# Batch 1's queries through scratch in device memory, its keys mixed two positions at a time, output weights in three tiles

## The chip, the cores and the metric

The kernel runs on one core of a Trainium2 chip. The metric is device time in microseconds (us) of one execution of the whole program; lower is better. A profile is one execution recorded by the hardware profiler, with the start and end of each engine's instructions. The engines are TensorE (PE in the profile; PEld is its weight load), VectorE (DVE), ScalarE (ACT), GpSimd (POOL) and SyncE (SP). SP computes nothing here and issues transfers; Pool issues others. Transfers run on 16 DMA engines that all queues share.

## What is computed

Four batches of eight heads, 768 positions, 64 channels a head. The positions of a head are cut into eight blocks of 96. An 8x8 matrix per head, made from `sort_net` by five rounds of normalising, mixes the blocks of keys and of values; then each block of queries attends to its own mixed block. The result, 3,072 rows of 512, goes through a gated feed-forward network.

```python
for _ in range(5):
    P = np.exp(P - np.max(P, axis=-1, keepdims=True))
    P = P / (np.sum(P, axis=-1, keepdims=True) + 1e-09)
    P = P / (np.sum(P, axis=-2, keepdims=True) + 1e-09)
k_sorted = np.einsum('bhij,bhjcd->bhicd', P, k_b)
v_sorted = np.einsum('bhij,bhjcd->bhicd', P, v_b)
scores = scale * np.matmul(q_b, k_sb.transpose(0, 1, 2, 4, 3))
attn = softmax(scores)
x = np.matmul(attn, v_sb)          # then 3072 x 512
g = x @ w_gate
out = (g / (1 + np.exp(-g)) * (x @ w_val)) @ w_out
```

## The kernel before

Matrix work is in bfloat16 with float32 sums. The feed-forward network goes in eight stages `ffn(0)` to `ffn(7)`, each over half a batch (384 rows): 12 gate tiles (line 385) and 12 value tiles (line 403) of four matmuls each, and, from stage 1 on, the output matmuls of the stage before (line 420, `outp`). The attention of the batches that follow is woven in: `merge` takes the stage's own steps in order, adds up a cost given to each by hand (0.65 or 0.87), and puts each side step in as soon as the sum has reached its due number. The order of TensorE and Pool is written out this way, so TensorE works strictly in order: what stands behind a waiting matmul waits too.

Batch 0 is done ahead of stage 0, by hand, and partly in stage 0. Batch 1 comes in stage 1: values mixed (`v_chunk`), keys and queries brought into channel-by-position form (`kq_chunk`, line 238), then `units(1, ...)`: each unit is the scores of two heads and half of the blocks (`scores`, line 293, matmuls on line 307), exponentials, attention times values, and the turn of the result. Units 0 to 3 of batch 1 stand in stage 1, units 4 to 7 in stage 2. Batches 2 and 3 form a pair whose keys are mixed together in stage 2.

How keys and queries of a batch get their form differs:

- Batch 0 loads one tile `qk0`: half of it holds keys with two positions of a block in the two halves of the partitions (`k0`), so one matmul mixes two positions (`k0_chunk`, 48 positions x 2 matmuls); queries are turned by a selecting matrix (`q0_chunk`).
- Batch 1 loads keys into the upper 64 partitions and queries into the lower 64 of one tile (`load_k(1)`, `load_q(1)`, lines 160 and 161). `kq_chunk` multiplies each of 96 positions by a matrix `rmix[1]` which holds the mix in its upper rows and an identity in its lower rows (line 536): 96 x 2 matmuls in chunks of 16 positions, six drains of 128x1024 from PSUM to `kqt`, by VectorE and ScalarE in turn. Keys and queries both come out in `kqt`.
- Batches 2 and 3 use `kq_chunk` for their keys alone. Their queries are copied by a casting transfer into scratch in device memory, 768 rows of 512 (`q_cast`, line 370), and brought back by one transposing transfer a batch on SP's queue (`q_dma`, line 375).

All large loads are issued by Pool in an order written out in lines 144 to 162: values and batch 0, gate and value weights in steps of 256 columns, values of batch 1, keys and queries of batch 1, and last the output weights as one transfer into one tile `wo_sb` (line 162). Pool then copies batch 1's values into another layout (line 124), and issues the loads of batches 2 and 3. SP's queue carries, in this order of use, the results (line 427), the transposing transfers of attention results from batch 1's unit 4 on (`x_dma`, line 366), and `q_dma`.

The score matmuls take their keys and queries from these places:

```python
k_sb, k_at, q_sb, q_at = ((kqts[b], 0, kqts[b], GI * C) if b < 2 else
                          (kqts["p"], (b - 2) * GI * C, kqts["q"], (b - 2) * GI * C))
```

Of the kernel before, what the change touches and what calls it, by code (L numbers as in the profile page):

```python
# [10 lines left out]
BF16 = mybir.dt.bfloat16  # L11
# [6 lines left out]
def kernel(  # L18
# [25 lines left out]
    R = H * NB  # L44

    k_nat = k.rearrange("b h (j c) d -> b (h j) c d", c=C)
    q_nat = q.rearrange("b h (j c) d -> b (h j) c d", c=C)
    v_nat = v.rearrange("b h (j c) d -> b (h j) c d", c=C)
    sn = sort_net.rearrange("b h i j -> (b h) i j")
    wg_dram = moe_w_gate.rearrange("(kc p) f -> p kc f", p=128)  # L50
# [1 line left out]
    wo_dram = moe_w_out.rearrange("(mc p) f -> p mc f", p=128)  # L52

    const = ctx.enter_context(tc.tile_pool(name="const", bufs=1))
    natp = ctx.enter_context(tc.tile_pool(name="natp", bufs=2))
    vnp = ctx.enter_context(tc.tile_pool(name="vnp", bufs=1))
    kqp = ctx.enter_context(tc.tile_pool(name="kqp", bufs=2))
    vtp = ctx.enter_context(tc.tile_pool(name="vtp", bufs=2))
# [12 lines left out]

    wg_sb = wpool.tile([128, NKC, DF], BF16)
    wv_sb = wpool.tile([128, NKC, DF], BF16)
    wo_sb = wpool.tile([128, NFC, DM], BF16)
    vch = const.tile([128, D * C + 32], BF16)
    nc.vector.memset(vch[:, D * C:], 0.0)
    vch3 = vch[:, 0:D * C].rearrange("p (d c) -> p d c", c=C)
# [2 lines left out]

    dram = ctx.enter_context(tc.tile_pool(name="dram", bufs=1, space=bass.MemoryType.DRAM))
    q_scr = [dram.tile([S, H * D], BF16, name=f"q_scr{b}") for b in range(2, B)]
    kq_tiles = {}
    v_tiles = {}

    def kq_tile(b):
        if b not in kq_tiles:
            kq_tiles[b] = natp.tile([128, C, D], BF16, name=f"kq{b}", tag="nat")
        return kq_tiles[b]

    def load_k(b, lo, hi):
        rows = highr if b else lowr
        nc.gpsimd.dma_start(out=kq_tile(b)[rows, lo:hi, :], in_=k_nat[b, :, lo:hi, :])

    def load_k_pair():
        kq_tiles["p"] = natp.tile([128, C, D], BF16, name="kp", tag="nat")
        for u in range(2):
            nc.gpsimd.dma_start(out=kq_tiles["p"][u * R:(u + 1) * R], in_=k_nat[2 + u])

    def load_q(b, lo, hi):  # L100
        rows = lowr if b else highr
        nc.gpsimd.dma_start(out=kq_tile(b)[rows, lo:hi, :], in_=q_nat[b, :, lo:hi, :])

    def load_v(b, lo, hi):
        if b // 2 not in v_tiles:
# [29 lines left out]
    halves = (lowr, highr)  # L135
    qk0 = natp.tile([128, C, D], BF16, name="qk0", tag="nat")
    k0 = qk0[:, 0:HC, :]
    q0 = [qk0[:, HC + t * QC:HC + (t + 1) * QC, :] for t in range(2)]
    q_runs = q.rearrange("b h (t r c) d -> b t r h (c d)", t=2, c=QC)

# [16 lines left out]
    load_v(1, 0, C)  # L157
    for m in range(1024, DF, 256):
        load_gv(m, m + 256)
    load_k(1, 0, C)  # L160
    load_q(1, 0, C)
    nc.gpsimd.dma_start(out=wo_sb, in_=wo_dram)

    rmix = {b: const.tile([128, 2, H, NB], BF16, name=f"rmix{b}") for b in (0, 1, "p")}
    for t in rmix.values():
# [62 lines left out]
    def kqt_tile(b):  # L228
        if b not in kqts:
            kqts[b] = kqp.tile([128, 2 * H2 * NB * C + 32], BF16, name=f"kqt{b}", tag="kqt")  # L230
        return kqts[b]
# [3 lines left out]
    def chunk_tile(name, n, tag):  # L235
        return pair_tile(name, tag) if n == 2 else bank_tile(name, tag)

    def kq_chunk(b, at, n, eng, tag):
        dst = kqt_tile(b)[:, 0:2 * GI * C].rearrange("p (n c) -> p n c", c=C)
        rm = rmix[b].rearrange("p a (g two) i -> p two (a g) i", two=2)  # L240
        tp = chunk_tile("tkq", n // 8, tag).rearrange("p (l n) -> p l n", n=2 * GI)
        for lc in range(n):
            for two in range(2):
                nc.tensor.matmul(tp[two * D:(two + 1) * D, lc, :],  # L244
                                 lhsT=kq_tiles[b][:, at + lc, :],
                                 rhs=rm[:, two], start=True, stop=True)
        drain(eng, dst[:, :, at:at + n], tp.transpose([0, 2, 1]))

# [6 lines left out]
                                 rhs=sel[:, two], start=True, stop=True)  # L255
        drain(eng, dst[:, :, :, at:at + n], tp.rearrange("p l g r -> p g r l"))

    def k0_chunk(at, n, eng, tag):
        dst = kqt_tile(0)[:, 0:GI * C].rearrange("p (n a c) -> p a n c", a=2, c=HC)
        rm = rmix[0].rearrange("p a (g two) i -> p two a g i", two=2)  # L260
        tp = chunk_tile("tk0", n // 8, tag).rearrange("p (l a n) -> p l a n", l=n, a=2)
        for lc in range(n):
            for two in range(2):
                nc.tensor.matmul(tp[two * D:(two + 1) * D, lc].rearrange("p a (g i) -> p a g i", g=H2),
                                 lhsT=k0[:, at + lc, :], rhs=rm[:, two], start=True, stop=True)
        drain(eng, dst[:, :, :, at:at + n], tp.rearrange("p l a n -> p a n l"))

    def v_chunk(b, at, n, eng, tag):
# [23 lines left out]

    def scores(b, u, tag):
        half, g = divmod(u, H2)
        k_sb, k_at, q_sb, q_at = ((kqts[b], 0, kqts[b], GI * C) if b < 2 else
                                  (kqts["p"], (b - 2) * GI * C, kqts["q"], (b - 2) * GI * C))
        if tag == "gen":
            wide = None
            pss = [bank_tile("qk"), bank_tile("qk")]
        else:  # L300
            wide = pair_tile("qk", tag).rearrange("p (two n) -> p two n", two=2)
            pss = [wide[:, 0], wide[:, 1]]
        for i4 in range(4):
            at = (g * NB + half * 4 + i4) * C
            for two in range(2):
                lo = two * D
                nc.tensor.matmul(pss[two][:, i4 * C:(i4 + 1) * C],  # L307
                                 lhsT=k_sb[lo:lo + D, k_at + at:k_at + at + 128],
                                 rhs=q_sb[lo:lo + D, q_at + at:q_at + at + C],
                                 start=True, stop=True)  # L310
        return wide, pss
# [11 lines left out]
    def qk(b, u, tag="b"):  # L323
        exps(b, u, *scores(b, u, tag))
# [44 lines left out]
    def q_cast(b):  # L369
        nc.gpsimd.dma_start(out=q_scr[b - 2].rearrange("s (h d) -> s h d", d=D),  # L370
                            in_=q[b].rearrange("h s d -> s h d"))

    def q_dma(b):
        dst = kqt_tile("q")[:, (b - 2) * GI * C:(b - 1) * GI * C]
        nc.sync.dma_start_transpose(out=dst.rearrange("p (g s) -> p g s", g=H2), in_=q_scr[b - 2])
# [37 lines left out]
    def outp(n, t3, part):  # L413
        b, half = divmod(n, 2)
        h_w = h_tiles[n]
        if part == 0:
            o_tiles[n] = bank_tile("o_ps", "x" if 2 <= n < 2 * B - 1 or n == 2 * B - 1 and t3 == 1 else "gen")
        o_ps = o_tiles[n]
        for m in range(part * 4, part * 4 + 4):
            nc.tensor.matmul(o_ps, lhsT=h_w[:, m, ts(t3, 128)], rhs=wo_sb[:, m, :],  # L420
                             start=(m == 0), stop=(m == NFC - 1))
        if part < 2:
            return
        o_sb = opool.tile([128, DM], FP32, name="o_sb", tag="o_sb")
        nc.scalar.copy(o_sb, o_ps)  # L425
        base = b * S + half * TW + t3 * 128
        nc.sync.dma_start(out=out[ds(base, 128), :], in_=o_sb)

    def out_halves(n, t3):
        b, half = divmod(n, 2)  # L430
        base = b * S + half * TW + t3 * 128
        for part, eng in ((0, "s"), (1, "v")):
            cols = slice(part * DM // 2, (part + 1) * DM // 2)
            o_ps = bank_tile("o_ps")[:, 0:DM // 2]
            for m in range(NFC):
                nc.tensor.matmul(o_ps, lhsT=h_tiles[n][:, m, ts(t3, 128)], rhs=wo_sb[:, m, cols],  # L436
                                 start=(m == 0), stop=(m == NFC - 1))
            o_sb = opool.tile([128, DM // 2], FP32, name="oh_sb", tag="oh_sb")
            drain(eng, o_sb, o_ps)
            nc.sync.dma_start(out=out[ds(base, 128), cols], in_=o_sb)  # L440
# [26 lines left out]
    def mix_rows(dst, rows, b):  # L467
        nc.vector.tensor_tensor(dst, mask[rows].unsqueeze(2).to_broadcast([R, H, NB]),
                                w_ps[rows, :, b].transpose([0, 2, 1]), op=ALU.mult)
# [9 lines left out]
    v_chunk(0, 32, 8, "v", "gen")  # L479
    v_chunk(0, 40, 16, "s", "b")  # L480
    v_chunk(0, 56, 8, "s", "gen")
    k0_chunk(0, 16, "v", "a")
    k0_chunk(16, 16, "s", "b")
    k0_chunk(32, 8, "v", "gen")
    k0_chunk(40, 8, "s", "gen")
    q0_chunk(0, 16, 8, "v", "a")
    fill(idle_ps, 4)
    qk(0, 0, "a")
# [1 line left out]
    for b in range(1, B):  # L490
        rows = halves[b % 2]
        mix_rows(rmix["p"][rows, b % 2] if b > 1 else rmix[1][rows, 0], rows, b)
    qk(0, 2, "gen")
    idle_ps = bank_tile("idle_ps")
    fill(idle_ps, 2)
# [37 lines left out]
    gate_out(0, 0, first[0])  # L533
    value_out(0, 0, first[1])
    gate_out(0, 1, first[2])
    nc.vector.tensor_copy(rmix[1][lowr, 1].rearrange("p h i -> p (h i)"), ident[lowr, lowr])
    man.__exit__(None, None, None)
    man = tc.manual_schedule(engines={ET.PE, ET.Pool})
    man.__enter__()
# [15 lines left out]
                    todo.append((at + t, lambda w=w, tag=tag: (av(b, w, tag), x_dma(b, w))))  # L555
        return todo

    def kqs(b, ats):
        return [(at, lambda n=n: (kq_chunk(b, n * 32, 16, "v", "b"), kq_chunk(b, n * 32 + 16, 16, "s", "a")))
                for n, at in enumerate(ats)]  # L560

    def vs(f, size, ats):
        return [(at, lambda m=m: f(1, m * size, size, "sv"[m % 2], "ba"[m % 2])) for m, at in enumerate(ats)]
# [39 lines left out]
    def q0_rest():  # L603
        q0_chunk(1, 0, 16, "s", "b")
        q0_chunk(1, 16, 8, "v", "a")

    merge(ffn(0), [(0.0, q0_rest)] + units(0, range(4, 8), (2.0, 6.6)))
    merge(ffn(1), vs(v_chunk, 16, (3.2, 3.9, 4.7, 5.5)) + kqs(1, (6.2, 8.2, 10.3))
          + units(1, range(4), (11.3, 16.4), (3.1, 2.5)))
    for s in range(4):  # L610
        copy_v(nc.gpsimd, 1, both, s)
    nc.vector.memset(kqt_tile("p")[:, 2 * GI * C:], 0.0)
    merge(ffn(2), units(1, range(4, 8), (0.0, 5.5)) + kqs("p", (13.0, 16.2, 19.4))
          + [(13.0, lambda: q_dma(2)), (16.4, lambda: q_dma(3))])
    merge(ffn(3), v_pairs([2.6 * n for n in range(4)]) + units(2, range(4), (9.8, 14.0)))
    merge(ffn(4), units(2, range(4, 8), (0.0, 8.0)))
# [38 lines left out]
```

## Time and profile before

| | |
|---|---|
| median of 3 runs | 248.91 us (248.74 to 250.26) |
| the profiled execution | 248.75 us, span of its instructions 246.8 us |
| granted TensorE clock | 1.000 |
| gate and value matmuls (lines 385, 403) | 756, 326 ns each |
| output matmuls (line 420) | 276, 379 ns each |
| mix of keys and queries, batch 1 (line 244) | 192 matmuls, 128x64 |
| the same, pair of batches 2 and 3 | 192 matmuls, 128x64 |
| drains of the mix, batch 1 | 3 on DVE of 1.219 us, 3 on ACT of 1.012 us |
| load of batch 1's keys, queries; output weights | 16.0, 18.9 and 24.9 us from issue to landing |

The span is the time from the first to the last instruction on the core. An engine's busy time is the sum of its instructions. In the slices, each digit is the busy share of a fortieth of the span in tenths. The chain of waits is followed back from the last instruction; what stands in it set the end. "DMA share" is the time that packets spent in the 16 engines, as a share of the stretch; it passes 1 where an engine has several packets under way.

### The profile page before, as it was taken

The numbers are of one execution on the slowest core, as the hardware profiler recorded it, in microseconds if no ns is written. First come the engines' busy times: TensorE is split into PE (matmuls) and PEld (weight loads), VectorE is DVE, ScalarE is ACT, GpSimd is POOL, SyncE is SP. The second block draws the span as 40 slices with busy tenths as digits, with TensorE's granted clock in tenths as the row PEclk, the third lists the DMA queues.
The fourth block names the chain that finished last, engine by engine and source line by source line (L and its number), as shares of the span: only waits on it lengthen the run. The fifth ranks groups of instructions, "written<-read, shape, count | busy, mean of one in ns | idle before, by whom it ended". The sixth has DMA issues, their size and how long they took to land.

```text
span 246.8 us, 6185 instructions
## 1 busy us (share of the span) xinstructions
PE 238.7 (97%) x2633; PEld 140.8 (57%) x2633; DVE 157.2 (64%) x332; ACT 110.7 (45%) x186; POOL 52.0 (21%) x45
## 2 busy tenths in 40 slices
PE   7799999999999999999999999999999999999994
PEld 5375666666555566655555655565555555555543
DVE  6786879886655685767656746754764585446700
ACT  3977653454454435364642642255245334322311
POOL 5994459950069200000000000000000000000000
PEclk9999999999999999999999999999999999999999
DMA  5999999999999395010121111112111211100122
GB/s 97 214 133 186 221 194 224 172 222 218 217 163 180 62 216 141 3 45 0 45 74 35 58 58 35 44 42 78 32 45 42 54 43 55 42 28 18 42 83 87
DMA packets 39578, 24.38 MB, mean 99 GB/s; under 512 B 27712, under 2 KB 35648, under 8 KB 39104
## 3 DMA queue, kind: packets, MB, share of 16 engines
q0 software_dynamic: 21376, 14.16, 39.6%
q1 hardware_dynamic: 18176, 9.84, 14.1%
q8 instruction: 20, 0.33, 0.5%
q14 instruction: 6, 0.05, 0.1%
HBM read 28.32 MB, written 7.86 MB: 147 GB/s over the span
## 4 chain that ended last, share of the span: by engine, by line
PE 84%; DVE 7%; ACT 3%; issue 3%; DMA 2%; DVEq 0%; ACTq 0%; POOLq 0%
PE v_ps L403 23%; PE o_ps L420 23%; PE g_ps L385 22%; PE av_ps L334 3%; PE tkq L244 3%; PE qk L307 3%; DVE gs_sb L395 2%; DMA v<-in_v_dram 2%; DVE h L408 1%; PE idle_ps L446 1%; PE tv L275 1%; PE o_ps L436 1%; DVE st L340 1%; PE x_ps L351 1%; ACT th_sb L393 1%
## 5 line engine op out<-in xcount | busy, mean ns | idle before, releaser
L395 DVE SCALAR_TENSOR_TENSOR gs_sb<-th_sb,g_ps 128x384 bf16<-128x384 bf16 x96 | 52.9, 551 | 51.0 <-ACT th_sb L393 48.3
L403 PE MATMUL v_ps<-xt,wv_sb 128*128 128x384 bf16 x380 | 77.3, 326 | 0.5 <-DVE gs_sb L395 0.4
L385 PE MATMUL g_ps<-xt,wg_sb 128*128 128x384 bf16 x376 | 76.7, 326 | 0.1
L393 ACT ACTIVATE th_sb<-g_ps 128x384 bf16<-128x384 f32 x96 | 47.1, 491 | 55.6 <-PE g_ps L385 53.2
L420 PE MATMUL o_ps<-wo_sb,h 128*128 128x512 bf16 x276 | 64.0, 379 | 0.0
L408 DVE SCALAR_TENSOR_TENSOR h<-v_ps,gs_sb 128x384 bf16<-128x384 f32 x96 | 53.4, 556 | 6.8
L403 PEld LDWEIGHTS <-wv_sb 128*128 128x128 bf16 x380 | 35.2, 97 | 24.2 <-issue 2.0
L385 PEld LDWEIGHTS <-wg_sb 128*128 128x128 bf16 x376 | 34.7, 97 | 23.5 <-issue 0.4
L420 PEld LDWEIGHTS <-h 128*128 128x128 bf16 x276 | 26.3, 98 | 28.9
L425 ACT COPY o_sb<-o_ps 128x512 f32<-128x512 f32 x23 | 13.5, 586 | 50.8 <-PE o_ps L420 50.8
L124 POOL COPY vch<-v 64x1536 bf16<-64x1536 bf16 (+2 forms) x11 | 28.7, 2654 | 21.8 <-DMA v<-in_v_dram 21.8
L320 ACT ACTIVATE e_all<-qk 96x768 bf16<-96x768 f32 x30 | 22.6, 802 | 7.7 <-PE qk L307 7.7
L340 DVE TENSOR_TENSOR st<-av_ps,r_sb 96x512 bf16<-96x512 f32 x32 | 21.7, 679 | 0.2
L334 PEld LDWEIGHTS <-e_all 96*128 96x128 bf16 x256 | 12.2, 98 | 4.9 <-ACT e_all L320 0.8
L334 PE MATMUL av_ps<-vt,e_all 96*128 96x65 bf16 x256 | 13.5, 194 | 0.0
L338 DVE RECIPROCAL r_sb<-av_ps 96x8 f32<-96x8 f32 x32 | 6.4, 199 | 8.1 <-PE av_ps L334 8.0
L222 DVE CAST vt<-tv 96x1024 bf16<-96x1024 f32 (+1 forms) x9 | 9.8, 1100 | 2.6 <-PE tv L285 1.6
L224 ACT CAST vt<-tv 96x1024 bf16<-96x1024 f32 (+1 forms) x9 | 9.2, 1032 | 2.9 <-PE tv L285 1.8
L446 PE MATMUL idle_ps<-warm_sb 128*128 128x512 bf16 x25 | 6.9, 382 | 0.0
L222 DVE COPY oh_sb<-o_ps 128x256 f32<-128x256 f32 x1 | 0.4, 425 | 9.3 <-PE o_ps L436 9.3
L370 POOL DMA_DIRECT2D q_scr<-in_q_dram x2 | 5.7, 3225 | 0.0
L122 ACT COPY vch<-v 64x768 bf16<-64x768 bf16 (+1 forms) x4 | 5.5, 1386 | 0.3 <-DMA v<-in_v_dram 0.3
(80 smaller groups left out, 134.8 us busy)
## 6 DMA issues: line engine op xcount, KB each, us to landing
out_dram<-o_sb SPq DMA_DIRECT2D x23, 256.0 KB, 2.0
v<-in_v_dram POOLq DMA_DIRECT2D x3, 768.0 KB, 19.9
wg_sb<-in_moe_w_gate_dram POOLq DMA_DIRECT2D x6, 256.0 KB, 9.9
wv_sb<-in_moe_w_val_dram POOLq DMA_DIRECT2D x6, 256.0 KB, 10.8
wo_sb<-in_moe_w_out_dram POOLq DMA_DIRECT2D x1, 1536.0 KB, 24.9
kp<-in_k_dram POOLq DMA_DIRECT2D x2, 768.0 KB, 15.3
q_scr<-in_q_dram POOLq DMA_DIRECT2D x2, 768.0 KB, 29.9
v<-in_v_dram POOLq DMA_DIRECT2D x2, 384.0 KB, 5.5
```

What stands on the lines that cost most here:

```text
L124: eng.tensor_copy(dst, src.transpose([0, 2, 1]))
L222: nc.vector.tensor_copy(dst, src)
L320: nc.scalar.activation(e_all[:, n:n + 2, 0:4 * C], wide[0:C, :, 0:4 * C], AF.Exp, scale=scale)
L334: nc.tensor.matmul(o[:, two, i4, :], lhsT=e[:, i4 * C:i4 * C + 128], rhs=vt[:, 2 * g + two, half * 4 + i4, :], start=True, stop=True)
L340: nc.vector.tensor_tensor(st.rearrange("p i two d -> p two i d"), o[0:C, :, :, 0:D], r_sb.to_broadcast([C, 2, 4, D]), op=ALU.mult)
L385: nc.tensor.matmul(g_ps, lhsT=wg_sb[:, kc, ts(m, 128)], rhs=xt[:, kc, :], start=(kc == 0), stop=(kc == NKC - 1))
L393: nc.scalar.activation(th_sb, g_ps, AF.Tanh, scale=0.5)
L395: nc.vector.scalar_tensor_tensor(gs_sb, th_sb, 1.0, g_ps, op0=ALU.add, op1=ALU.mult)
L403: nc.tensor.matmul(v_ps, lhsT=wv_sb[:, kc, ts(m, 128)], rhs=xt[:, kc, :], start=(kc == 0), stop=(kc == NKC - 1))
L408: nc.vector.scalar_tensor_tensor(h_tiles[n][:, m, :], v_ps, 0.5, gs_tiles.pop(m), op0=ALU.mult, op1=ALU.mult)
L420: nc.tensor.matmul(o_ps, lhsT=h_w[:, m, ts(t3, 128)], rhs=wo_sb[:, m, :], start=(m == 0), stop=(m == NFC - 1))
L425: nc.scalar.copy(o_sb, o_ps)
```

## The change

Batch 1's queries no longer pass TensorE. A casting transfer copies them to scratch (`q1_scr`, eight heads of 768 x 64), and `q1_dma` asks for a transposing transfer for each head on SP's queue, into a tile `q1t` of channels by positions. It is called ahead of `ffn(0)`. Batch 1's keys are loaded as batch 0's are, into `k1`, and mixed by the same function, now `k_chunk(b, ...)`: 48 positions x 2 matmuls in three chunks of 16. Its side steps are due at 7.2 and 9.2 in place of 6.2, 8.2 and 10.3. `rmix[1]` holds the mix in both halves, so one more `mix_rows` stands in place of the copy of the identity. The output weights are three tiles, loaded by three transfers. The pool `natp` has one buffer in place of two.

```diff
-    natp = ctx.enter_context(tc.tile_pool(name="natp", bufs=2))
+    natp = ctx.enter_context(tc.tile_pool(name="natp", bufs=1))
...
-    wo_sb = wpool.tile([128, NFC, DM], BF16)
+    wo_sb = [wpool.tile([128, 4, DM], BF16, name=f"wo{n}") for n in range(3)]
...
+    q1_scr = dram.tile([H, S, D], BF16, name="q_scr1")
...
+    k1 = const.tile([128, HC, D], BF16)
+    q1t = const.tile([128, H2, S], BF16)
...
-    load_k(1, 0, C)
-    load_q(1, 0, C)
-    nc.gpsimd.dma_start(out=wo_sb, in_=wo_dram)
+    nc.gpsimd.dma_start(out=q1_scr.rearrange("h (t s) d -> (h t) (s d)", t=2),
+                        in_=q[1].rearrange("h (t s) d -> (h t) (s d)", t=2))
+    for a, rows in enumerate((highr, lowr)):
+        nc.gpsimd.dma_start(out=k1[rows], in_=k_nat[1, :, a * HC:(a + 1) * HC, :])
+    for n in range(3):
+        nc.gpsimd.dma_start(out=wo_sb[n], in_=wo_dram[:, n * 4:(n + 1) * 4, :])
...
-    def k0_chunk(at, n, eng, tag):
-        dst = kqt_tile(0)[:, 0:GI * C].rearrange("p (n a c) -> p a n c", a=2, c=HC)
-        rm = rmix[0].rearrange("p a (g two) i -> p two a g i", two=2)
+    def k_chunk(b, at, n, eng, tag):
+        dst = kqt_tile(b)[:, 0:GI * C].rearrange("p (n a c) -> p a n c", a=2, c=HC)
+        rm = rmix[b].rearrange("p a (g two) i -> p two a g i", two=2)
...
-                                 lhsT=k0[:, at + lc, :], rhs=rm[:, two], start=True, stop=True)
+                                 lhsT=(k0, k1)[b][:, at + lc, :], rhs=rm[:, two], start=True, stop=True)
...
-        k_sb, k_at, q_sb, q_at = ((kqts[b], 0, kqts[b], GI * C) if b < 2 else
+        k_sb, k_at, q_sb, q_at = ((kqts[b], 0, q1t.rearrange("p g s -> p (g s)") if b else kqts[b],
+                                   0 if b else GI * C) if b < 2 else
...
+    def q1_dma():
+        for h in range(H):
+            g, two = divmod(h, 2)
+            nc.sync.dma_start_transpose(out=q1t[two * D:(two + 1) * D, g, :], in_=q1_scr[h])
...
-            nc.tensor.matmul(o_ps, lhsT=h_w[:, m, ts(t3, 128)], rhs=wo_sb[:, m, :],
+            nc.tensor.matmul(o_ps, lhsT=h_w[:, m, ts(t3, 128)], rhs=wo_sb[part][:, m % 4, :],
...
+    mix_rows(rmix[1][lowr, 1], lowr, 1)
...
-    nc.vector.tensor_copy(rmix[1][lowr, 1].rearrange("p h i -> p (h i)"), ident[lowr, lowr])
+    nc.vector.memset(kqt_tile(1)[:, GI * C:GI * C + 32], 0.0)
...
+    def k1s(ats):
+        return [(ats[0], lambda: (k_chunk(1, 0, 16, "v", "b"), k_chunk(1, 16, 16, "s", "a"))),
+                (ats[1], lambda: k_chunk(1, 32, 16, "v", "b"))]
...
+    q1_dma()
     merge(ffn(0), [(0.0, q0_rest)] + units(0, range(4, 8), (2.0, 6.6)))
-    merge(ffn(1), vs(v_chunk, 16, (3.2, 3.9, 4.7, 5.5)) + kqs(1, (6.2, 8.2, 10.3))
+    merge(ffn(1), vs(v_chunk, 16, (3.2, 3.9, 4.7, 5.5)) + k1s((7.2, 9.2))
           + units(1, range(4), (11.3, 16.4), (3.1, 2.5)))
```

The functions that served batch 1's old load (`kq_tile`, `load_k`, `load_q`) go, and `kq_chunk`, now for the pair alone, is called `kp_chunk`. The line numbers of the changed kernel differ: its score matmuls are on line 300, `q1_dma` on 369, `x_dma` on 359, `q_dma` on 373, the results on 425.

More of the change, by code (lines that the diff above doesn't have):

```diff
@@ L46 @@
     k_nat = k.rearrange("b h (j c) d -> b (h j) c d", c=C)
-    q_nat = q.rearrange("b h (j c) d -> b (h j) c d", c=C)
     v_nat = v.rearrange("b h (j c) d -> b (h j) c d", c=C)
@@ L82 @@
     q_scr = [dram.tile([S, H * D], BF16, name=f"q_scr{b}") for b in range(2, B)]
+    q1_scr = dram.tile([H, S, D], BF16, name="q_scr1")
     kq_tiles = {}
     v_tiles = {}
[L86 to L93, printed above, removed]
     def load_k_pair():
@@ L98, in load_k_pair @@
             nc.gpsimd.dma_start(out=kq_tiles["p"][u * R:(u + 1) * R], in_=k_nat[2 + u])
-    def load_q(b, lo, hi):
-        rows = lowr if b else highr
-        nc.gpsimd.dma_start(out=kq_tile(b)[rows, lo:hi, :], in_=q_nat[b, :, lo:hi, :])
     def load_v(b, lo, hi):
@@ L236, in chunk_tile, with kp_chunk @@
         return pair_tile(name, tag) if n == 2 else bank_tile(name, tag)
-    def kq_chunk(b, at, n, eng, tag):
-        dst = kqt_tile(b)[:, 0:2 * GI * C].rearrange("p (n c) -> p n c", c=C)
-        rm = rmix[b].rearrange("p a (g two) i -> p two (a g) i", two=2)
+    def kp_chunk(at, n, eng, tag):
+        dst = kqt_tile("p")[:, 0:2 * GI * C].rearrange("p (n c) -> p n c", c=C)
+        rm = rmix["p"].rearrange("p a (g two) i -> p two (a g) i", two=2)
         tp = chunk_tile("tkq", n // 8, tag).rearrange("p (l n) -> p l n", n=2 * GI)
@@ L244, in kq_chunk @@
                 nc.tensor.matmul(tp[two * D:(two + 1) * D, lc, :],
-                                 lhsT=kq_tiles[b][:, at + lc, :],
+                                 lhsT=kq_tiles["p"][:, at + lc, :],
                                  rhs=rm[:, two], start=True, stop=True)
@@ L435, in out_halves @@
             for m in range(NFC):
-                nc.tensor.matmul(o_ps, lhsT=h_tiles[n][:, m, ts(t3, 128)], rhs=wo_sb[:, m, cols],
+                nc.tensor.matmul(o_ps, lhsT=h_tiles[n][:, m, ts(t3, 128)], rhs=wo_sb[m // 4][:, m % 4, cols],
                                  start=(m == 0), stop=(m == NFC - 1))
@@ L481 @@
     v_chunk(0, 56, 8, "s", "gen")
[L482 to L485, printed above, removed]
+    k_chunk(0, 0, 16, "v", "a")
+    k_chunk(0, 16, 16, "s", "b")
+    k_chunk(0, 32, 8, "v", "gen")
+    k_chunk(0, 40, 8, "s", "gen")
     q0_chunk(0, 16, 8, "v", "a")
@@ L556, in units, with kps @@
         return todo
-    def kqs(b, ats):
-        return [(at, lambda n=n: (kq_chunk(b, n * 32, 16, "v", "b"), kq_chunk(b, n * 32 + 16, 16, "s", "a")))
+    def kps(ats):
+        return [(at, lambda n=n: (kp_chunk(n * 32, 16, "v", "b"), kp_chunk(n * 32 + 16, 16, "s", "a")))
                 for n, at in enumerate(ats)]
+    def k1s(ats):
+        return [(ats[0], lambda: (k_chunk(1, 0, 16, "v", "b"), k_chunk(1, 16, 16, "s", "a"))),
+                (ats[1], lambda: k_chunk(1, 32, 16, "v", "b"))]
     def vs(f, size, ats):
@@ L612 @@
     nc.vector.memset(kqt_tile("p")[:, 2 * GI * C:], 0.0)
-    merge(ffn(2), units(1, range(4, 8), (0.0, 5.5)) + kqs("p", (13.0, 16.2, 19.4))
+    merge(ffn(2), units(1, range(4, 8), (0.0, 5.5)) + kps((13.0, 16.2, 19.4))
           + [(13.0, lambda: q_dma(2)), (16.4, lambda: q_dma(3))])
```

## The prediction

> **What bounds the kernel now.** I read the page first: the busy shares and the slices in time.
>
> ```profile
> PE 238.7 (97%) x2633; PEld 140.8 (57%) x2633; DVE 157.2 (64%) x332; ACT 110.7 (45%) x186; POOL 52.0 (21%) x45
> ...
> PE   7799999999999999999999999999999999999994
> ...
> DMA  5999999999999395010121111112111211100122
> ```
>
> TensorE has no slice with a hole in it, and the last chain of waits is 84% TensorE. So only two things can move the time: fewer TensorE instructions, or something that makes TensorE wait. The transfer engines are full for the first 13 slices (80 us) and nearly empty after them, so before 80 us a new transfer meets others.
>
> Next, the chain of waits around batch 1's mix, 54 to 69 us (columns: start, length, what).
>
> ```profile
> 55.34 1.13 PE tkq L244 x64
> ...
> 58.96 1.15 PE tkq L244 x64
> 60.11 0.02 issue
> 60.13 1.01 ACT kqt L224
> ...
> 68.21 0.34 PE qk L307 x8
> ```
>
> The mix is three groups of 64 matmuls, 1.13 to 1.15 us each, 17.7 ns a matmul. TensorE then loses about 1.0 us to the last drain before the first batch 1 scores (61.2 us in the order of time). The fourth scores of the batch start at 68.21.
>
> Then transfers, issue to landing, and their queue in order of time.
>
> ```profile
> kq<-in_k_dram POOLq DMA_DIRECT2D x1, 768.0 KB, 16.0
> ...
> kqtq<-q_scr SPq DMA_TRANSPOSE x2, 6.0
> ```
>
> ```profile
> 84.35 3.34 SPq L375 DMA_TRANSPOSE kqtq<-q_scr  x1
> ...
> 89.72 3.16 SPq L375 DMA_TRANSPOSE kqtq<-q_scr  x1
> ```
>
> Last, stretches chosen so that one kind of packet fills them (columns at the end: granted clock, DMA share, GB/s).
>
> ```profile
> 72.00:74.00 2.00, 2.00 (x23) 1.36 (x22) 2.00 (x6) 0.49 (x1) 2.00 (x2) 1.00 2.44 161
> ```
>
> ```profile
> 87.00:88.00 1.00, 1.00 (x14) 0.73 (x13) 0.75 (x2) 0.49 (x1) 0.00 (x0) 1.00 1.28 291
> ...
> 97.00:98.00 1.00, 1.00 (x38) 0.77 (x33) 1.00 (x2) 0.43 (x1) 0.00 (x0) 1.00 0.69 262
> ```
>
> At 87 to 88 only the batch 2 query transpose moves, in 256-byte packets. (768 rows x 1,024 B in such pieces are 3,072 packets; with 384 for each of the 20 activation transposes and a packet per output row this gives 17,024 of the queue's 18,176.) 291 kB/us are 1,137 packets/us, 71 per engine: one each 14.1 ns, in flight 1.28 x 14.1 = 18 ns. At 97 to 98 one output tile moves, 128 packets of 2,048 B: 0.69 x 16 us / 128 = 86 ns each. A line through these two has 0.038 ns per byte and 8.3 ns left at 2 bytes. At 72 to 74 the casting copies of batches 2 and 3 write 128-byte packets: 1,258/us, 12.7 ns apart per engine, 31 ns in flight.
>
> **What the change really issues.** The eight transposes have a source of 768 rows of 64 bfloat16. The program built from the changed kernel does not list them as transposes. The other two transposing lines (359 and 373) stand in it as DmaTransposeAnt; line 369 stands eight times as a plain copy:
>
> ```
> L369 DMACopy q1t<-q_scr_108 64x768x1 [waits DMASW3_49]
> L369 DMACopy q1t<-q_scr_108 64x768x1 x6
> L369 DMACopy q1t<-q_scr_108 64x768x1 [waits DMAHW0_49]
> ```
>
> Its access pattern on the source steps 64 elements between neighbours, last dimension 1. So each is 64 x 768 = 49,152 pieces of 2 bytes, all eight 393,216; over 16 engines 24,576 each. That is the cost of this change. The Trainium skill, "DMA: Bandwidth & Descriptors", section "DMA Transpose (X-bar)", says that a DRAM source narrower than 128 elements can fall back to a rearranged pattern with inefficient descriptors, and its rules for authors that a strided last dimension costs a descriptor per element: the rule against this change.
>
> **Part by part.**
>
> *Key mix.* 48 positions x 2 matmuls instead of 96 x 2: 96 fewer x 17.7 ns = 1.7 us of TensorE; three drains fewer (one DVE of 1.22, two ACT of 1.01), off the path. The last chunk is placed at 9.2 instead of 10.3 with the scores still at 11.3, so the 1.0 us wait can go. Gain at most 2.7 us, all ahead of the new wait and so swallowed by it; I take 0.
>
> *Scratch copy.* It takes the place in the Pool queue of the old key load, issued at 26.9 with 16.0 us to landing, the same 768 KB written: ready at 43. (The old query load took 18.9 us; bounds 40 to 48.)
>
> *The eight copies.* Price of a 2-byte packet per engine, bounded by rows: not under 8.3/1.28 = 6.5 ns (the line's end, with the transposes' overlap), 160 us for all; not over 31 ns (the casts' time in flight, with no overlap), 762 us. I take 14.1 ns, because it is the distance between packets in the nearest row: same queue, small reads from the same kind of scratch in device memory, and the casts with half the bytes written show nearly the same 12.7, so distance hardly shrinks with size. 24,576 x 14.1 = 347 us. The issuing queue says much the same: (3.34 + 3.16)/2 us for 3,072 packets are 1.06 ns each, 416 us for 393,216. By the page's "Why small descriptors are slow" (about 3 cycles over a 32-byte beat, at the 850 MHz it gives for the fabric) a packet is 4 cycles, 4.7 ns, 116 us, an estimate that would make the time 376 us. "VectorE: DVE Perf Modes", "The three transpose paths", calls such a copy 19 times slower than the hardware transpose; 19 x the 6.0 us above is 114 us, nearly the same estimate. The rows shown here do not confirm such a short distance, since 256 bytes take 14.1 ns.
>
> *Sharing.* From 43 to 80 us the engines still carry Pool's loads (output weights, batches 2 and 3), full by the slices. Both queues use the same 16 engines: 37 us to add, bounds 0 and 37.
>
> *Who waits.* In the built program TensorE's scores wait head by head, in order; the last wait is in the fourth scores (heads 6 and 7), which start at 68.21 now. Behind it in TensorE's order stands everything else: from 68.21 to the end of the span 246.8 are 178.6 us, plus 1.95 around the span (the profiled execution took 248.75; the median of the runs is 248.91), 180.5 in all. On SP the first output tiles and batch 1's activation transposes stand behind the eight copies; they are wanted only after the wait, 0.
>
> *Small things.* Output weights in three and keys in two transfers: same bytes, three more Pool issues at 0.35 to 0.54 us, and the third waits for a value-weight load (22.9 + at most 13.6 = 36.5) before Pool's batch 1 value copies start, now at 34.0: up to 2.5 us late, for the batch 1 value mix that ends by 51, ahead of the big wait, 0. One more DVE mix of 0.22 us, one copy turned into a memset: 0. The pool with one buffer: the pair's keys still wait for the same reader (done at 27, issue at 45), 0.
>
> Sum: 43 + 347 + 37 + 180.5 = **607 us**.
>
> **The rivals.**
>
> *Dear elements (0.17).* A 2-byte write could cost what the casts' packets show in flight: 24 ns with the transposes' overlap (31/1.28), 595 us, total 856; 31 ns without any, 1,023. For it: the small writes in flight longest are the casts. Against: they still overlap 2.4 times.
>
> *Cheap elements (0.09).* Under 6.5 ns, or Pool's loads wholly beside them: at 6.5 ns 420 us with sharing, 383 without. For it: 8.3 ns at size nothing; against: the 12.7 and 14.1 rows, and the 1.06 ns of issue.
>
> *Hidden, faster (0.02).* The copies land before the fourth scores need them: eight heads in 68.2 - 43 = 25 us, which decides at 25 us/24,576 = 1.0 ns per packet, or if the chip carried line 369 out as real transposes (6,144 packets x 14.1 ns / 16 = 5.4 us). Then the mix's 2.7 us show: 246.0. Against: the listing, and the lowest bound above is 6.5 ns. A hundredth is left for no difference.
>
> **How the numbers follow.** The forecast case (0.71) spans 6.5 to 18 ns (18 is the 256-byte packet's time in flight, not overlapped: 442 us), 420 to 703 us. The 8-in-10 range takes it whole and reaches into the dear case up to its overlapped end, 420 to 856: half of the dear case (0.09) lies above, the cheap case and the two last (0.12) below. Over 1% (2.5 us) faster 0.02, within 0.01, slower 0.97; a change of 1% is what this kernel's runs can tell from none.
>
> **What would show it.** The issues should list line 369 as DMA_DIRECT2D with 49,152 packets each and the packet count should rise by about 393,000; TensorE should have one long gap in pieces, at batch 1's first four scores, released by the q1t transfer, nothing in it, with 178 us of unchanged work after it; queue 1's packets over that gap give the ns per element. It is wrong if the gap is under 100 us, if TensorE waits longest elsewhere (output weights, Pool), or if the copies are paced by SP's issue rather than by the engines.

## The result and the profile after

The changed kernel takes 749.24 us (median of 4 runs, 744.72 to 753.45) against 248.88 us: a ratio of 3.008, 95% interval 3.000 to 3.016. The profiled execution took 751.51 us, its span is 749.5. A run more than 1.5% above the fastest of its kernel counts as slow and is left out of the ratios, which below leaves e1_whole one run (279.43 us), e2_wo_one two and e9_early3 three.

The page of the changed kernel: busy shares, the slices, the transfer queues.

```profile
PE 242.2 (32%) x2537; PEld 141.0 (19%) x2537; DVE 156.3 (21%) x332; ACT 109.0 (15%) x184; POOL 53.2 (7%) x48
...
PE   8983000000000000030000000000006999999998
...
PEclk9997555555555555565555555555557999999999
DMA  8999999999999999999999999999991601111101
GB/s 150 205 193 162 56 1 1 2 2 2 2 2 2 2 2 2 2 2 2 2 2 2 2 2 2 2 2 2 2 2 29 134 30 51 50 47 46 50 29 71
DMA packets 433002, 25.16 MB, mean 34 GB/s; under 512 B 421104, under 2 KB 429040, under 8 KB 432624
```

TensorE runs 96 matmuls fewer than before, is busy for about as long (242.2 us, 238.7 before) and stands idle for two thirds of the span. Through all that time the 16 transfer engines are full, and once Pool's loads are done they move 1 to 2 GB/s. The packets rose from 39,578 to 433,002, by 393,424: the 393,216 pieces of 2 bytes and a few of other kinds.

TensorE's two largest waits (us in total, times, longest), and the issues of lines 369 and 373 (KB each where given, us to landing):

```profile
PE qk L300 <- DMA q1t<-q_scr: 497.8, 8, 79.3
PE tv L267 <- POOL vch L111: 2.0, 1, 2.0
```

```profile
q1t<-q_scr SPq DMA_DIRECT2D x8, 96.0 KB, 127.8
...
kqtq<-q_scr SPq DMA_TRANSPOSE x2, 6.1
```

There is one wait for each head. Line 369 is carried out as DMA_DIRECT2D, not as a transpose, beside line 373, which is one. A chain of waits shows the pace (in it the page calls these transfers an unknown queue):

```profile
60.06 1.83 PE o_ps L418 x8
61.90 79.21 another core or an unknown queue
141.48 61.42 another core or an unknown queue
203.41 60.32 another core or an unknown queue
264.01 60.70 another core or an unknown queue
...
508.33 60.41 another core or an unknown queue
569.26 3.52 PE o_ps L418 x8
```

The heads land 61 us apart: 61.1 us / 3,072 pieces per engine = 19.9 ns a piece. The first took 97.5 us from its issue at 43.6 to 141.1, 36.4 more than the distance of the others, which come when Pool's loads are done.

### The profile page after: what moved, and what is told of

The parts are those of the page before. It is cut to its first block, busy times and chain, and to the rows that moved or that the text cites. A ratio compares the mean times of both kernels' runs of the same rounds, so it can differ in the third digit from the quotient of the medians.

```text
span 749.5 us, 6010 instructions
## 1 busy us (share of the span) xinstructions
PE 242.2 (32%) x2537; PEld 141.0 (19%) x2537; DVE 156.3 (21%) x332; ACT 109.0 (15%) x184; POOL 53.2 (7%) x48
## 2 busy tenths in 40 slices
DMA packets 433002, 25.16 MB, mean 34 GB/s; under 512 B 421104, under 2 KB 429040, under 8 KB 432624
## 4 chain that ended last, share of the span: by engine, by line
another core or an unknown queue 66%; PE 28%; DVE 2%; issue 1%; DMA 1%; ACT 1%; POOL 0%; DVEq 0%; ACTq 0%; POOLq 0%
PE o_ps L418 8%; PE v_ps L401 8%; PE g_ps L383 8%; PE qk L300 1%; PE av_ps L327 1%; DMA v<-in_v_dram 1%; DVE vt L214 1%; DVE gs_sb L393 1%; PE tkq L236 0%; POOL vch L111 0%; PE o_ps L434 0%; PE x_ps L344 0%; PE tk L256 0%; DVE kqt L214 0%
## 5 line engine op out<-in xcount | busy, mean ns | idle before, releaser
L300 PE MATMUL qk<-q1t,kqt 64*128 64x96 bf16 x64 | 3.9, 234 | 497.8 <-DMA q1t<-q_scr 497.8
L300 PEld LDWEIGHTS <-kqt 64*128 64x128 bf16 x128 | 3.8, 100 | 501.5 <-issue 446.6
L418 PE MATMUL o_ps<-wo,h 128*128 128x512 bf16 x276 | 65.7, 386 | 0.0
L214 DVE COPY xt<-x_ps 128x384 bf16<-128x384 bf16 x9 | 3.1, 350 | 241.2 <-PE x_ps L344 241.2
```

The lines of the kernel that those rows point to most:

```text
L214: nc.vector.tensor_copy(dst, src)
L300: nc.tensor.matmul(pss[two][:, i4 * C:(i4 + 1) * C], lhsT=k_sb[lo:lo + D, k_at + at:k_at + at + 128], rhs=q_sb[lo:lo + D, q_at + at:q_at + ...
```

## The experiments

### One part undone, one part doubled

**e1_whole** undoes the element copies alone: scratch of 768 rows of 512, one transposing transfer.

```diff
...
-        for h in range(H):
-            g, two = divmod(h, 2)
-            nc.sync.dma_start_transpose(out=q1t[two * D:(two + 1) * D, g, :], in_=q1_scr[h])
+        nc.sync.dma_start_transpose(out=q1t, in_=q1_scr)
```

> One part of the change undone: the scratch holds batch 1's queries as 768 rows of 512 and one transposing transfer brings them back, as batches 2 and 3 do it. My theory (the whole loss is the 393,216 two-byte packets, the rest of the change is worth a little): the 500 us of waits for q1t are gone, and 246 to 249 us remain, 96 key matmuls fewer (1.7 us) against up to 2.5 us of later value copies. Rival (something else of the change is dear as well: the split output weights, the later Pool work, the copy through scratch itself): 252 us or more, with a wait for wo, for vch or for q1t in the profile. This kernel's scratch copy writes 6,144 pieces of 128 B where the changed kernel's writes rows, and so takes some 2.5 us more of Pool's time.

Measured 284.17 us (median of 6 runs, 279.43 to 286.3) against 249.01. Of the 500 us nearly all are gone, but 30 (by the fastest run) to 35 (by the median) are left: the rival was right that something else is dear. TensorE's waits and the transfer's landing in e1_whole:

```profile
PE qk L300 <- DMA q1t<-q_scr: 17.4, 1, 17.4
PE o_ps L416 <- DMA wo<-in_moe_w_out_dram: 13.7, 1, 13.7
PE tv L267 <- POOL vch L111: 2.2, 1, 2.2
```

```profile
q1t<-q_scr SPq DMA_TRANSPOSE x1, 49.6
```

The same kind of transfer that lands in 6 us for batch 2 takes 49.6 here. The packets of the stretch 62 to 82 us:

```profile
DMA packets 1480, 2.41 MB, mean 121 GB/s; under 512 B 1286, under 2 KB 1306, under 8 KB 1306
...
q0 software_dynamic: 735, 2.22, 88.7%
q1 hardware_dynamic: 745, 0.19, 58.2%
```

Pool's queue (q0) and SP's (q1) sent 735 and 745 packets: one for one. But Pool's 735 carry 2.22 MB and SP's 0.19 MB, because 174 of them (1,480 - 1,306) are of 8 KB and more: packets of 12,288 B of the big loads of batches 2 and 3, each some 0.93 us under way. Most of the rest are 128-byte pieces of the casting copies behind those loads. Beside a queue of big packets, turns of one each hold the small packets back. The Trainium skill, "DMA: Bandwidth & Descriptors", section "Queues, rings and completion order", says that an engine goes round its queues packet by packet; these counts agree. They are not the whole of it: from 78 to 82 us only 15 of 225 packets are big, and yet no more than 113 of the transposing transfer go out, where alone, at 87 to 88 us of the kernel before, 1,136 went out in 1 us. Why the engines without a big packet are slow too, no run shows.

**e4_half** brings heads 0 to 3 by one transposing transfer and leaves heads 4 to 7 as element copies.

```diff
...
-        for h in range(H):
+        nc.sync.dma_start_transpose(out=q1t[:, 0:2, :], in_=q1_low)
+        for h in range(H // 2, H):
```

> The changed kernel with heads 0 to 3 brought by one transposing transfer out of a second scratch of 768 rows of 256, and only heads 4 to 7 by the 2-byte copies. Theory (each head costs 60.7 us of packets, plus the sharing with Pool's loads once, about 37 us, and the rest is unchanged): the last head lands at 43 + 37 + 4 x 60.7 = 323 us, and with 180 us behind it the time is about 503 us; 749 - 503 = 246. Rival (the wait is a fixed one, such as a queue that has to drain or a clock that has to come back, and does not go with the number of packets): over 600 us.

Measured 516.79 us in one run: half the pieces remove 232 of the 500 us, so the wait goes with the number of pieces and is no fixed cost. It is 14 us over the 503; SP issued one element copy (at 43.1) ahead of the transposing transfer (45.6), which then met 2-byte pieces as well as Pool's loads and took 95 us of SP's queue. That the 14 come from there was not tried apart.

### The price of a piece

**e3_prices** adds eight copies behind the last matmul of e1_whole, each into the same tile, so that each waits for the one before. Two of them, A and C:

```diff
+    nc.sync.dma_start(out=lin[0:64, 0:768], in_=rows64[0:768].rearrange("s d -> d s"))
...
+    nc.sync.dma_start(out=lin[0:64, 0:1536].rearrange("p (s e) -> p s e", e=2), in_=rows128[0:768].rearrange("s (p e) -> p s e", e=2))
```

> The kernel with one transposing transfer, and behind its last matmul eight further copies into a tile that is no longer needed, one after another, each alone on the engines. They add time on purpose; the output is computed in full. Read: issue to landing of each. A, one head as in the changed kernel (49,152 pieces of 2 B): 61 us by the changed kernel's profile. B, source neighbours 4 B apart in place of 128 B: 61 if the scattered read is not the cause, clearly less if it is. C, 49,152 pieces of 4 B: 61 if a packet has a fixed price, 2 x 61 if a byte has. D, 2 B pieces from SBUF: 61 if reading device memory is not the cause, less if it is. E, 24,576 pieces over 8 partitions, 3,072 per engine on half of the engines: 61 if each engine paces its own packets, 31 if one generator paces all of them. F, 49,152 pieces over 16 partitions: 61 by both. G, 6,144 pieces of 64 B: 384 per engine, 8 us at the 2 B price, 5 to 6 us at the 14 ns that 256 B packets show; H, 1,536 pieces of 256 B: 96 per engine, 2 us over the fixed part at most. My theory now: a fixed price per packet and engine of some 20 ns, whatever the size below 256 B, raised over the 14 ns because the write of a piece shorter than some unit is dearer; rival: one generator of descriptors makes one in 1.24 ns for all engines.

SP's queue in order of time (start, length of the issue); A to H are lines 634 to 648, and a copy's time is the distance to the next start.

```profile
284.23 0.74 SPq L634 DMA_DIRECT2D h<-q_scr  x1
...
348.02 0.56 SPq L636 DMA_DIRECT2D h<-q_scr  x1
412.00 0.61 SPq L638 DMA_DIRECT2D h<-q_scr  x1
442.93 0.63 SPq L640 DMA_DIRECT2D h<-h  x1
506.30 0.84 SPq L642 DMA_DIRECT2D h<-q_scr  x1
610.92 0.63 SPq L644 DMA_DIRECT2D h<-q_scr  x1
715.53 0.65 SPq L646 DMA_DIRECT2D h<-q_scr  x1
721.33 0.61 SPq L648 DMA_DIRECT2D h<-q_scr  x1
```

Near neighbours (B, 64.0 us) and SBUF as the source (D, 63.4) cost the same as A (63.8): the scattered read of device memory is not the cause. C is the surprise: the same number of pieces with twice the bytes takes 30.9 us, half. E, with half the pieces on half of the engines (DMA share 0.98, for F 1.97), takes the same 104.6 us as F: no single generator of descriptors sets the pace, which for E would give half of F. SP's own issue of 49,152 pieces lasts 0.56 to 0.74 us. G, 6,144 pieces of 64 B, took 5.7 us to landing and H, 1,536 of 256 B, 4.0: less than the 2 B price asks for. And 104.6 in place of 61, for 8 and 16 partitions, was expected by neither theory.

**e7_prices2** does the same with six other copies (lines 634 to 644).

```diff
+    nc.sync.dma_start(out=lin[0:64, 0:1536].rearrange("p (n two) -> p n two", two=2)[:, :, 0], in_=rows64[0:768].rearrange("s d -> d s"))
+    nc.sync.dma_start(out=lin[:, 0:384], in_=rows128[0:384].rearrange("s d -> d s"))
...
+    nc.sync.dma_start(out=rows64[0:768].rearrange("s d -> d s"), in_=lin[0:64, 0:768])
```

> Again the kernel with one transposing transfer, with other copies behind its last matmul, one after another (they add time on purpose). Measured before: 49,152 pieces of 2 B took 63.7 us over 64 partitions, from near or far, from device memory or from SBUF; 30.9 us as 4 B pieces; 104.6 us over 16 partitions. Theory W: the write of less than 4 bytes into SBUF is a read and a write of a word, and the engines that write to the same few partitions get into each other's way. Rival N: pieces are dear because neighbours fall into the same 4-byte word one after another. A, 2 B pieces 4 B apart at their destination: 64 us by W, 31 by N. B, 128 partitions: under 64 by W with crowding (40 to 50), 64 without. C, 32 partitions: between 64 and 105 by crowding. D, 4 B pieces over 16 partitions, 24,576 (half the number): 52 us if crowding holds for 4 B too (at half of 104.6), 15 if only the short write crowds. E, 49,152 pieces of 8 B: 31 us if a packet has a fixed price from 4 B up. F, 49,152 pieces of 2 B into device memory from SBUF (this overwrites scratch that is no longer used): 64 if the short write is dear there too, 31 if it is SBUF's.

```profile
276.65 0.75 SPq L634 DMA_DIRECT2D h<-q_scr  x1
...
340.54 0.41 SPq L636 DMA_DIRECT2D h<-q_scr  x1
382.02 0.66 SPq L638 DMA_DIRECT2D h<-q_scr  x1
445.72 0.59 SPq L640 DMA_DIRECT2D h<-q_scr  x1
469.28 0.63 SPq L642 DMA_DIRECT2D h<-q_scr  x1
501.08 0.65 SPq L644 DMA_DIRECT2D q_scr<-h  x1
```

A, pieces 4 bytes apart: 63.9 us, so neighbours in one word are not the reason; what is left is the 2-byte piece itself. B, 128 partitions: 41.5. C, 32 partitions: 63.7, as with 64, where crowding alone should have given more. D, half the number in 4 B over 16 partitions: 23.6, between the two expectations: 4 B pieces get dearer there too, but by less. E, 8 B: 31.8, the 4 B price. F, from SBUF into device memory: 100.9 us to landing. The prices follow when some 2 us of fixed part are taken off a copy that runs alone (an estimate: 63.7 us alone against 61.1 in a row, 41.5 against 39.8 by e10_pairs below). From 4 to 8 bytes a packet has one price over 64 partitions, some 9.5 ns per engine (G's 64 bytes fit it: 3.7 us / 384 = 9.6 ns), and over 16 partitions 14 ns for 4 bytes. A 2-byte piece costs about twice that over 64 or 32 partitions, 20 ns; 12.9 ns over 128, some 33 over 16 or 8. The source changes nothing (A, B and D of e3_prices), the destination does, so the price belongs to the write side. Reads and writes were shortened together in every copy, though, so that the short write alone makes the doubling is argued. Why it is dear inside the engine, and why the price goes in such steps, no run shows.

**e10_pairs** takes that price back into the changed kernel: the same 393,216 pieces, two heads to a copy, so that 128 partitions are written.

```diff
...
-        for h in range(H):
-            g, two = divmod(h, 2)
-            nc.sync.dma_start_transpose(out=q1t[two * D:(two + 1) * D, g, :], in_=q1_scr[h])
+        for g in range(H2):
+            nc.sync.dma_start(out=q1t[:, g, :], in_=q1_scr[:, g * 128:(g + 1) * 128].rearrange("s p -> p s"))
```

> The changed kernel with the same 393,216 pieces of 2 bytes, but two heads to a copy: four plain copies that write all 128 partitions in place of eight that write 64 (the scratch is 768 rows of 512 for that). Theory: the price of a 2-byte piece is set at the write side and falls with the number of partitions that the engines write to; alone it was 41.5 us over 128 partitions and 63.7 over 64, so (41.5 - 2)/3,072 = 12.9 ns. Then 45 + 37 + 24,576 x 12.9 ns + 180.5 = 579 us, 170 less than the changed kernel. Rival (a 2-byte piece has one price and the measurement alone does not carry over to the kernel, where the wait is for the reads or the queue): 745 us or more.

Measured 580.5 us in one run, 579 expected. TensorE's waits end at 158.46, 238.05, 317.76 and 396.98, that is 79.5 us a copy or 12.9 ns a piece:

```profile
PE qk L300 <- DMA q1t<-q_scr: 326.2, 4, 96.5
```

The loss is the number of pieces times a price that goes with the partitions written.

### What is left when the transfer is a real transpose

**e5_after_q1** holds Pool's big loads until the transfer has landed and puts the small-packet copies first; a copy of 16 elements on Pool is what waits.

```diff
+    q_cast(2)
+    q_cast(3)
+    q1_dma()
+    seen = const.tile([1, 16], BF16)
+    nc.gpsimd.tensor_copy(seen, q1t[0:1, H2 - 1, S - 16:S])
     load_k_pair()
     load_v(2, 0, C)
     load_v(3, 0, C)
-    q_cast(2)
-    q_cast(3)
...
-    q1_dma()
```

> The kernel with one transposing transfer for batch 1 lost 35 us: the transfer took 49.6 us to land where batch 2's takes 6. Theory now: each DMA engine takes packets from its two queues in turn, so while Pool's loads of batches 2 and 3 run in packets of 12,288 B (some 0.9 us each) a 256 B packet of the transfer goes out only about once per big packet. Here Pool copies batches 2 and 3's queries first (128 B packets) and issues those big loads only when the transfer has landed. Theory: the transfer lands 15 to 20 us after its start at 45 (it still meets the output weights, 1 KB packets), so at 60 to 65; the wait for it falls from 17 us to under 5, the wait for the output weights from 14 us to under 2; the time is 247 to 254. Rival (a transposing transfer is slow beside any other traffic, whatever its packets, or the output weights are late for another reason): the waits stay, 265 us or more.

Measured 253.76 us, ratio 1.017 (1.011 to 1.022). In e5_after_q1 the wait for the transfer falls to 0.9 us and the one for the output weights is gone; the transfer lands in 19.9 us:

```profile
PE tv L267 <- POOL vch L111: 2.6, 1, 2.6
...
PE qk L300 <- DMA q1t<-q_scr: 0.9, 1, 0.9
```

```profile
q1t<-q_scr SPq DMA_TRANSPOSE x1, 19.9
```

Keeping the transfer away from the big loads was worth 26 us of e1_whole's 30 (its fastest run) or 30 of its 35 (medians). The small packets still meet the output weights, and the first scores start at 64.7 in place of 61.2.

Four more kernels look for the rest; their edits are orders of issue.

**e2_wo_one**: e1_whole with the output weights as one transfer.

```diff
...
-    for n in range(3):
-        nc.gpsimd.dma_start(out=wo_sb[n], in_=wo_dram[:, n * 4:(n + 1) * 4, :])
+    nc.gpsimd.dma_start(out=wo_sb, in_=wo_dram)
```

> The kernel with one transposing transfer, and the output weights again as one transfer into one tile. If the split of the output weights delays Pool's copies of batch 1's values through the two further issues and their waits for older loads (theory), this is 1 to 2.5 us faster than with three tiles, unless the first output matmuls at 57 us then wait for the whole tile. If the split costs nothing (rival), the two agree within 0.5 us.

287.31 us, ratio 1.137 (1.129 to 1.145). The wait for the value copies is gone, but the output matmuls wait for the whole tile, as the expectation allowed for:

```profile
PE o_ps L415 <- DMA wo_sb<-in_moe_w_out_dram: 20.4, 1, 20.4
PE qk L299 <- DMA q1t<-q_scr: 13.3, 1, 13.3
```

That is 6.7 us more for the output weights and 4.1 less for the transfer, which TensorE waits for behind them; with the 2.2 us for the value copies the waits add up to 33.7 us here and 33.3 in e1_whole. The runs, 281.35 to 294.21 us, overlap with those of e1_whole, so whether the split helps beside a slowed queue is not shown.

**e6_shift**: e5_after_q1 with `vs(v_chunk, 16, (5.0, 5.7, 6.5, 7.3)) + k1s((8.6, 9.8))`.

> The same, with batch 1's value and key chunks put some 1.5 to 2 us of main work later (5.0 to 7.3 for 3.2 to 5.5, and 8.6 and 9.8 for 7.2 and 9.2), because TensorE waits 2.2 us for Pool's value copies, which the scratch copy and the split output weights delay. Theory: that wait falls to under 0.7 us and the time by 1 to 2 us against the kernel without the shift. Rival: the wait only moves, to the drains ahead of the first scores, and the two agree within 0.5 us.

254.67 us, ratio 1.020 (1.015 to 1.025), 0.9 us more than e5_after_q1: the time did not fall as the theory had it, and the rival was right that the wait only moves, though not where to. The wait for the value copies went, and the wait for q1t grew from 0.9 to 4.9 us, because the transfer still lands at 64.7.

**e8_early** and **e9_early3**: the scratch copy ahead of the last gate and value weights, the big loads held; one output weight tile or three.

```diff
     load_v(1, 0, C)
+    nc.gpsimd.dma_start(out=q1_scr.rearrange("s (h d) -> s h d", d=D),
+                        in_=q[1].rearrange("h s d -> s h d"))
     for m in range(1024, DF, 256):
...
```

> One transposing transfer for batch 1, its scratch copy issued 5 to 6 us earlier in Pool's order (ahead of the last two pairs of gate and value weights), the output weights in one transfer again, and the big loads of batches 2 and 3 held until the transfer has landed. Theory (what was left over the kernel before was the late scratch copy and the late value copies): the transfer lands by 57, TensorE does not wait for it, and the 96 matmuls fewer show: 246 to 249 us. Rival (the scratch copy's bytes push the weights behind it, which TensorE then waits for, or the output weights as the last of the loads come at 58 or later): 250 to 254, with a wait for wg, wv or wo of 2 us or more.

> The same with the output weights as three tiles. Theory: the first third lands 5 us or more ahead of the whole, so no output matmul waits, but the value copies start 2 to 3 us later and the value mix waits 1 to 2 us: within 1.5 us of the kernel with one transfer, on either side. Rival (the split is worth what it promises): 2 us or more faster than with one transfer.

e8_early took 254.95 us, ratio 1.020 (1.015 to 1.025): the rival, and 1 us beyond its range. e9_early3 has a median of 257.4 and a ratio of 1.022 (1.017 to 1.027). In e8_early TensorE does not wait for q1t any more, but for what was pushed back:

```profile
PE g_ps L380 <- DMA wg_sb<-in_moe_w_gate_dram: 2.9, 1, 2.9
PE v_ps L398 <- DMA wv_sb<-in_moe_w_val_dram: 2.4, 1, 2.4
```

The transfers are the limit of the first 60 us here: what was put earlier made another later. The fastest three runs of e9_early3 average 254.9 us, the fastest five of e8_early 254.6: within the 1.5 us that its theory gave, so one tile or three makes no difference that these runs show.

**e11_split**: the kernel before with the output weights in three tiles and nothing else.

```diff
-    wo_sb = wpool.tile([128, NFC, DM], BF16)
+    wo_sb = [wpool.tile([128, 4, DM], BF16, name=f"wo{n}") for n in range(3)]
```

> The kernel before with one part of the change alone: the output weights as three tiles and three transfers. Theory: two further Pool issues and their waits for older loads put Pool's value copies of batch 1 some 2 to 3 us later, TensorE waits for them by 1 to 2 us, so 250 to 251.5. Rival (same bytes in the same order, the copies have slack): within 0.5 us of before, or faster because the first third lands earlier.

250.0 us, ratio 1.005 (1.003 to 1.006), that is 1.1 us by the averages. Pool's value copies begin at 36.2 in place of 34.0, as expected, but TensorE waits only 0.4 us for them; where the other 0.7 us went is not settled.

None of these beats the kernel before. Whether the key mix by itself gains was not tried: its matmuls carried the queries too, so it has no meaning without another way for them.

## Why the prediction was right, and where its size was off

- *The transposes are plain copies of 393,216 pieces, and TensorE waits for them head by head.* Right: there are 8 waits of 497.8 us in all, line 369 is a DMA_DIRECT2D, and the packet count rose by 393,424.
- *Scratch ready at 43.* Right: SP could issue the first copy at 43.6.
- *Sharing with Pool's loads, 37 us.* The first head took 36.4 more than the rest, the first copy of e10_pairs 34.6. That the size came out is in part luck. Pool's packets ended at 90 us, not at 80, and the pieces did not stand behind them but went out beside them: 18,773 by 90 us, worth 23 us at 19.9 ns. So the loads cost about 23 us of the 46; some 7 more are the 6,034 pieces beyond one head that were out when the first landed, and the rest is not accounted for (an estimate from the counts of queue 1).
- *The rest, 180.5 us behind the last head.* Right within 2.3 us: 751.51 - 568.7 = 182.8 in the profiled execution; 1.7 us of the difference are eight output matmuls right behind the last wait, which took 3.52 us in place of 1.83 after the clock had fallen.
- *14.1 ns a piece, 347 us.* The mis-sized term: 19.9 ns and 489 us. These 142 us are nearly all of the miss (749.24 - 607); the other terms add up to 2 us in the profiled execution. The step that failed is "distance hardly shrinks with size", by which the row of 256-byte packets, those of a real transpose, was taken as the nearest. In plain copies the distance is 9.5 ns at 4 and 8 bytes. But a piece of 2 bytes costs about twice as much, and its price depends on the partitions written, which no row of the profile before could show. Its second witness, 1.06 ns of SP's issue a packet, did not carry over either: SP issues 49,152 pieces in 0.56 to 0.74 us. The dear rival was nearer in kind: a piece is under way for some 38 ns (19.9 ns times a DMA share of about 1.9), longer than the 31 ns of the casts, but more of them overlap than the 1.28 that it took. The forecast case ended at 18 ns and the dear one began at 24. The measured price lies between them in neither, and the range held it because it ran on through the gap; that part is luck.
- *The page's 4.7 ns and the factor 19.* The Trainium skill, "VectorE: DVE Perf Modes", section "The three transpose paths", warns of a plain copy that transposes by its strides; it names a large stride at the destination, and here the large stride is at the source. Its factor falls short here, and so do the 4.7 ns: eight heads at 61.1 us are 489 us against 6.0 for the hardware's transpose of the same bytes, a factor of 81.
- *Paced by the engines, not by SP's issue.* Supported by e3_prices, E against F and SP's short issue; that the write side sets the price, by its A, B and D (the source does not matter), by e7_prices2, B and F (the destination does), and by e10_pairs.
- *Hidden, faster.* It fails at its own condition, 1.0 ns a piece; and e1_whole, e5_after_q1 and e8_early show that a real transpose would not have been free either. The prediction put its cost at 5.4 us; beside the big packets it was 49.6, and in the best order 253.76 us stand against the 246.0 hoped for.
- *Split weights, up to 2.5 us of later value copies.* The copies began at 37.6 in place of 34.0, 3.6 us later, and TensorE waited 2.0 us for them, swallowed as said; the split alone costs 1.1 us.

## What to carry to other kernels

Look at what a transposing call became in the built program. Here a source of 64 columns turned it into one piece per element, where sources of 256 and 512 columns stayed transposes. The price is the pieces per engine times some 10 ns at 4 and 8 bytes, and 13 to 33 ns at 2 bytes, by the partitions written. A small-packet transfer that is wanted soon should not share the engines with a load in packets of 12 KB: the queues take turns by packets and not by bytes. In a stage that the transfers limit, a way around TensorE through device memory pays with the stage's scarce resource to save 1.7 us of another.

## What was not expected of the hardware

The granted TensorE clock falls to 0.50 while TensorE waits (slices of 5 in the line of the clock), and the matmuls right after a wait run at half speed, 3.52 us for eight in place of 1.83. And 49,152 pieces of 2 bytes written from SBUF into device memory, 128 bytes apart, took 100.9 us, against 63.4 from SBUF into 64 partitions of SBUF.
